# Second MoE stage: a GpSimd drain between scatters, an earlier load of the rare path's flag, and branch hints

## The chip, the cores and the metric

The kernel runs on one core of one Trainium2 chip. Its time is the device time of one execution in microseconds (us), lower is better. Engines: TensorE (PE, with its weight loads PEld), VectorE (DVE), ScalarE (ACT), GpSimd (POOL), SyncE (SP). SyncE and GpSimd issue the DMA transfers.

## What is computed

A gated linear recurrence over 768 steps, then two mixture-of-experts stages over the same 3072 rows of 384. Only the second one and the end of the program matter here:

```python
def _moe2_ref(x, w_skip, w_gate, w1, w2) -> np.ndarray:
    ...
    skip_score = x @ w_skip
    do_compute = skip_score > 0
    out = x.copy()
    ...
    for e in range(E):                      # 8 experts
        mask = e_idx == e
        ...
        h = np.maximum(xc[mask] @ w1[e], 0.0)
        y[mask] = gate_w[mask, None] * (h @ w2[e])
    out[do_compute] = xc + y
    return out.astype(np.float32)
```

## The kernel before

The recurrence is done first, in chunks of 128 steps; the first MoE stage follows and writes its rows to the output in DRAM; the second MoE stage updates those rows in place.

The second stage (`Moe2`, line 1476) works in 8 slots, numbered 0 to 7 here, one expert each, on one tile of 128 rows that were gathered from the output. `Rows128.run` (line 1288) writes out the order of every slot by hand, and `tc.manual_schedule()` (line 1567) keeps it: each engine runs its instructions in the order in which the program names them. A slot does, in this order: `ahead(s)` (loads), the first half of the first product, the first half of the second product of the slot before, the second half of the first product, the transposes, the second half of the second product of the slot before, and `finish(s - 1)`. Between them the weights of the next slot are split into a high and a low part in eight pieces, ScalarE making the high part (line 144) and VectorE the low one by a subtraction (line 145). So the scatter of slot s stands near the end of slot s + 1, and the last slot's two half products follow behind the loop.

`Moe2.finish` (line 1497) makes `z` on VectorE (line 1500, a tile with two buffers) and issues the scatter of `z` to the output on GpSimd (line 1502). Every scatter waits for the landing of the one before, since both write the output. There are eight scatters, one for each slot; no other transfer is issued on GpSimd in the stage.

`Moe2.run` (line 1506) takes one `hook`, which its `ahead` calls at slot 2, behind that slot's loads: the function `remaining` (line 1807), a few VectorE instructions that count what does not fit into the eight slots and leave it as an integer in `tot`.

Behind the stage a rare path stands in the program, for data that do not fit: the recurrence once more step by step, more slots of both stages. It is some thousands of instructions long. The branch around it is

```python
        with tc.If(flag(tot, 0, 4) > 0):
```

(line 1830). `flag` (line 1827) is `nc.values_load`, which makes all five engines load `tot` into a register (line 1828) behind nine instructions that each wait for one or two semaphores; then each engine branches. With these data `tot` is 0, so every engine jumps over the rare path to the end of the program. [...]

Of the kernel before, what the change touches and what calls it, by code (L numbers as in the profile page):

```python
# [16 lines left out]
PSUM = bass.MemoryType.PSUM  # L17
DRAM = bass.MemoryType.DRAM
IDX = bass.IndirectOffsetOnAxis

B, H, S, D = 4, 8, 768, 48
N, DM, E, F = 3072, 384, 8, 1024
# [32 lines left out]
KP, SP = (3, 4, 5), ()  # L55
# [43 lines left out]
class Weights:  # L99
# [3 lines left out]
    W = 3 * F + 8 * DW  # L103
# [12 lines left out]
    def load_rows(self, s, w1, w2, idx, wg=None):  # L116
        for o, w, n in ((3 * F + 8 * DM, wg, 8 * RC), (0, w1, 3 * F), (3 * F, w2, 8 * DM)):
            if w is not None:
                self.nc.gpsimd.indirect_dma_start(
                    out=self.raw[s % 2][:, o:o + n], out_offset=None, in_=w, in_offset=IDX(ap=idx, axis=0),  # L120
                    bounds_check=E * 128 - 1, oob_is_err=False)
# [1120 lines left out]
class Rows128:  # L1242
# [45 lines left out]
    def run(self, slots, src, ahead, fill, finish, x=None, side=lambda: None):  # L1288

        slots = list(slots)  # L1290
        x = x or self.turn(src(slots[0]))
        prev = None
        for i, s in enumerate(slots):
            ahead(s)
            f = fill(s)
            h0 = self.half1(s, x, 0)
            side()
            if prev is not None:
                self.half2(s - 1, prev, 0)
            next(f, None)  # L1300
            next(f, None)
            side()
            h1 = self.half1(s, x, 1)
            if i + 1 < len(slots):
                x = self.turn(src(s + 1))
            hs = [self.turn_h(h0)]
            next(f, None)
            next(f, None)
            side()
            if prev is not None:  # L1310
                finish(s - 1, self.half2(s - 1, prev, 1))
            hs.append(self.turn_h(h1))
            emit(f)
            side()
            prev = hs
        self.half2(s, prev, 0)
        finish(s, self.half2(s, prev, 1))


class Moe1:  # L1320
# [34 lines left out]
    def gather_rows(self, out, c, n=N):  # L1355
        self.nc.gpsimd.indirect_dma_start(
            out=out, out_offset=None, in_=self.k.x0[0:n], in_offset=IDX(ap=self.R.idx[:, c:c + 1], axis=0),
            bounds_check=n - 1, oob_is_err=False)
# [48 lines left out]
    def finish(self):  # L1407
        emit(self.side)
# [7 lines left out]
    def store(self, c, ps):  # L1416
# [5 lines left out]
        nc.gpsimd.indirect_dma_start(  # L1422
            out=k.out, out_offset=IDX(ap=R.idx[:, c:c + 1], axis=0), in_=y, in_offset=None,
            bounds_check=N - 1, oob_is_err=False)
# [51 lines left out]
class Moe2:  # L1476
# [20 lines left out]
    def finish(self, s, ps):  # L1497
# [4 lines left out]
        nc.gpsimd.indirect_dma_start(  # L1502
            out=k.out, out_offset=IDX(ap=k.idx2[:, s:s + 1], axis=0), in_=z, in_offset=None,
            bounds_check=N - 1, oob_is_err=False)

    def run(self, slots, load, loaded=False, hook=None):


        slots = list(slots)
        s0, end = slots[0], slots[-1] + 1  # L1510
        if not loaded:
            for s in range(s0, min(s0 + 2, end)):
                load(s)
                self.gather(s)
            emit(self.W.split(s0))
        else:
            for s in range(s0 + E - 2, end):
                self.gather(s)

        def ahead(s):  # L1520
            if s + 2 < end:
                if not loaded:
                    self.gather(s + 2)
                load(s + 2)
            if hook is not None and s == s0 + 2:
                hook()

        def fill(s):
            return self.W.split(s + 1) if s + 1 < end else iter(())

        self.rows.run(slots, lambda s: self.xg[s % E], ahead, fill, self.finish)
# [3 lines left out]
def tile_lru_attention_moe_moe(  # L1535
# [19 lines left out]
    nc = tc.nc  # L1555
    k = Env()
# [10 lines left out]
    with tc.manual_schedule():  # L1567
# [71 lines left out]
        W = Weights(nc)  # L1639
# [58 lines left out]
        tot = ct([1, 2], "tot2", I32)  # L1698
        R2 = Router(nc, k, const2, rt1, SUB1, "b")

        xq = [xg0[:, 0], xg0[:, 1], *(ct([128, DM], f"xq{i}") for i in range(2, E - 2))]
# [115 lines left out]
            v.tensor_tensor(rest[:, 0:1], rest[:, 0:1], rest[:, 1:2], op=ALU.add)  # L1817
            v.tensor_copy(tot[:, 0:1], rest[:, 0:1])

        def second_moe(ctx):  # L1820
            Moe2(nc, tc, k, W, ctx, xq, gather2).run(range(E), lambda s: W.load(s, v1, v2, s), loaded=True, hook=remaining)

        for moe in (first_moe, second_moe):
            with ExitStack() as c:
                moe(c)

        def flag(x, i, n):
            return nc.values_load(x[:, i:i + 1], min_val=0, max_val=n)

        with tc.If(flag(tot, 0, 4) > 0):  # L1830
            with tc.If(flag(k.okn, 0, 2 * 128 * G) < 2 * 128 * G):
                attention_steps(nc, tc, k)
                with ExitStack() as c:
                    sp = c.enter_context(tc.tile_pool(name="sl_s", bufs=1))
                    ps = c.enter_context(tc.tile_pool(name="sl_q", bufs=1, space=PSUM)).tile([128, 512], F32, name="sps")
                    R1.reset()
                    emit(R1.batch1(0, BT[0], ps))
                    emit(R1.batch1(BT[0], BT[1], ps))
                    emit(early(lambda shape, nm, dt: sp.tile(shape, dt, name=nm), ps[:, 256:]))
                    emit(split0())  # L1840
                for moe in (first_moe, second_moe):
                    with ExitStack() as c:
                        moe(c)
            with tc.If(flag(R1.tot, 3, 2) > 0):
                with ExitStack() as c:
                    m1 = Moe1(nc, tc, k, W, R1, c, xg0)
                    emit(R1.late_tables(m1.acc, c.enter_context(tc.tile_pool(name="m1s", bufs=2)), FIX1, SUB1 - FIX1))
                    with tc.If(flag(R1.tot, 0, 1) > 0):
                        m1.run_more(
                            range(NS1, NSMAX1), lambda s: W.load_rows(s, w1, w2, R1.wix[:, s + NZ1:s + NZ1 + 1], k.wg))  # L1850
                    for i, zs in ((1, range(NZ1, NZ1 + 2)), (2, range(NZ1 + 2, NZMAX1))):
                        with tc.If(flag(R1.tot, i, 1) > 0):
                            m1.run_more_small(
                                zs, lambda z: W.load_rows(z, w1, w2, R1.wix[:, NSMAX1 + z:NSMAX1 + z + 1], k.wg))
                    emit(batch2(FIX1, SUB1, m1.side_ps, None))
            with ExitStack() as c:
                m2 = Moe2(nc, tc, k, W, c, xq, gather2)
                rp = c.enter_context(tc.tile_pool(name="r3", bufs=1))
                pp = c.enter_context(tc.tile_pool(name="r3p", bufs=1, space=PSUM))
                n2 = overflow(nc, k, R2, tot, rp, pp)  # L1860
                for s0 in range(0, J2, 6):
                    with tc.If(n2 > s0):
                        m2.run(
                            range(E + s0, E + min(s0 + 6, J2)),
                            lambda s: W.load_rows(s, v1, v2, k.wix2[:, s - E:s - E + 1]))
# [106 lines left out]
```

## Time and profile before

| | us |
|---|---|
| median of 3 runs (lowest, highest) | 719.96 (714.34, 720.8) |
| the profiled execution | 717.57 |
| its span, first to last instruction | 715.8 |

Busy time in the span: TensorE 610.0 us (85%), VectorE 579.1 (81%), ScalarE 431.4 (60%), GpSimd 208.7 (29%). These are sums over stages with different limits, so they do not say what the end of the program costs. Busy time leaves out what a sequencer does by itself: waits for semaphores, loads of registers, branches and drains. Such instructions stand in the views under the name of their engine with a q (POOLq, DVEq, PEldq, SPq).

### The profile page before, as it was taken

What the parts mean: (1) busy time and instruction counts of PE and PEld (TensorE: products, weight loads), DVE (VectorE), ACT (ScalarE), POOL (GpSimd) and SP (SyncE); (2) the same over time, 40 slices, a digit from 0 to 9 for tenths busy, and PEclk for the clock granted to TensorE, in tenths of its full rate; (3) what the DMA queues carried; (4) which work ended last, traced back from release to release, by engine and by line L of the source; (5) the groups of instructions that cost most, each with busy time, mean ns of one, the idle gap of its engine ahead of it and who ended that gap; (6) DMA issues with size and microseconds to landing.
All of it is one profiled execution on the core that took longest, in us unless ns stands there. A gap on an engine that the chain in (4) does not pass through costs nothing.

```text
span 715.8 us, 13793 instructions
## 1 busy us (share of the span) xinstructions
PE 610.0 (85%) x5015; PEld 527.7 (74%) x5015; DVE 579.1 (81%) x1391; ACT 431.4 (60%) x863; POOL 208.7 (29%) x300
## 2 busy tenths in 40 slices
PE   0788886607999999998698999999999999799991
PEld 0454444406888888887598899999999997588890
DVE  5999999998999989998679666667766678699970
ACT  7767786634656656654543655566555566588860
POOL 6200000002223322234144534445454442601110
PEclk9999998965899999999789999999999999999996
DMA  6759864102998989767250211551111185578800
GB/s 224 285 191 288 289 200 114 66 0 65 244 255 227 229 218 232 194 175 242 91 202 23 66 46 38 224 210 50 34 52 41 33 334 228 214 276 312 312 18 11
DMA packets 39833, 117.21 MB, mean 164 GB/s; under 512 B 10172, under 2 KB 26186, under 8 KB 35404
## 3 DMA queue, kind: packets, MB, share of 16 engines
q1 hardware_dynamic: 22892, 66.37, 29.9%
q0 software_dynamic: 13984, 45.94, 20.5%
q10 hardware_dynamic: 2880, 3.93, 1.8%
q8 instruction: 41, 0.67, 0.4%
q14 instruction: 36, 0.29, 0.1%
HBM read 116.84 MB, written 16.52 MB: 186 GB/s over the span
## 4 chain that ended last, share of the span: by engine, by line
PE 32%; DMA 7%; issue 6%; DVE 6%; POOL 1%; ACT 1%; POOLq 0%; ACTq 0%; DVEq 0%
PE hps L1387 13%; PE yps L1434 13%; DMA out_dram<-z,idx 6%; PE yps L1283 1%; PE hps L1263 1%; DMA P<-in_w_dram,wix 1%; DVE wlo L145 1%; PE xtp L1371 1%; DVE w L145 1%; POOL xq L1704 1%; DMA xq<-out_dram,idx 1%; PE acc L1033 0%; DVE hl L1394 0%; DVE ro L1051 0%; PE yp L644 0%
## 5 line engine op out<-in xcount | busy, mean ns | idle before, releaser
L145 DVE TENSOR_TENSOR wlo<-wraw,whi 128x768 fp32r<-128x768 f32 (+1 forms) x95 | 82.4, 904 | 11.6 <-ACT whi L144 10.8
L145 DVE TENSOR_TENSOR w<-P,w 128x768 fp32r<-128x768 f32 (+1 forms) x95 | 82.6, 906 | 8.7 <-ACT w L144 7.9
L462 POOL DMA_DIRECT2D X<-X x36 | 17.8, 501 | 241.9 <-DVE X L521 226.4
L1394 DVE SCALAR_TENSOR_TENSOR hl<-hps,hh 128x512 fp32r<-128x512 f32 x48 | 33.1, 689 | 54.3 <-ACT hh L1393 47.5
L274 PE MATMUL m<-sq,idn 128*128 128x288 f32 x112 | 39.0, 476 | 42.1 <-ACT sq L267 42.1
L144 ACT ACTIVATE w<-P 128x768 fp32r<-128x768 f32 (+1 forms) x95 | 70.8, 800 | 2.8 <-DMA P<-in_w_dram,wix 2.8
L144 ACT ACTIVATE whi<-wraw 128x768 fp32r<-128x768 f32 (+1 forms) x95 | 71.0, 803 | 0.0
L1393 ACT ACTIVATE hh<-hps 128x512 fp32r<-128x512 f32 x48 | 28.7, 599 | 67.6 <-PE hps L1387 51.0
L274 PEld LDWEIGHTS m<-sq,idn 128*128 128x128 f32 x112 | 21.9, 214 | 54.9 <-ACT sq L267 29.3
L377 DVE TENSOR_TENSOR t<-P,n 128x288 f32<-128x288 f32 x127 | 58.9, 464 | 2.8 <-DVE n L327 0.2
L1422 POOL DMA_INDIRECT out_dram<-y,idx x26 | 30.9, 1187 | 101.9 <-ACT y L1421 98.2
L570 PE MATMUL sc<-X 48*128 48x128 f32 x768 | 56.0, 295 | 0.0
L570 PEld LDWEIGHTS sc<-X 48*128 48x128 f32 x768 | 50.8, 203 | 5.0 <-issue 3.1
L1434 PE MATMUL yps<-w,hh 128*128 128x394 f32 x192 | 51.0, 346 | 0.0
L1387 PE MATMUL hps<-xh,w 128*128 128x256 f32 x288 | 45.1, 289 | 2.6 <-ACT xh L1373 1.4
L1387 PEld LDWEIGHTS hps<-xh,w 128*128 128x128 f32 x288 | 39.7, 194 | 3.5 <-ACT xh L1373 1.8
L574 DVE TENSOR_TENSOR sm<-sc,tri 128x512 f32<-128x512 f32 x48 | 32.1, 685 | 10.8 <-PE sc L570 10.8
L382 DVE TENSOR_TENSOR P<-t 128x144 f32<-128x144 f32 x127 | 39.3, 309 | 0.1
L642 PE MATMUL yp<-sm,v 128*64 128x128 f32 (+1 forms) x384 | 36.2, 277 | 0.0
L1434 PEld LDWEIGHTS yps<-w,hh 128*128 128x128 f32 x192 | 34.9, 189 | 0.0
L274 PE MATMUL u<-sq,idn 128*128 128x288 f32 x112 | 34.9, 438 | 0.0
L1434 PE MATMUL yps<-whi,hh 128*128 128x394 f32 x96 | 33.6, 350 | 0.0
(365 smaller groups left out, 1743.9 us busy)
## 6 DMA issues: line engine op xcount, KB each, us to landing
P<-in_w2t_dram SPq DMA_DIRECT2D x8, 1536.0 KB, 6.7
P<-in_v_dram SPq DMA_DIRECT2D x8, 1536.0 KB, 7.3
wraw<-in_v_dram SPq DMA_DIRECT2D x8, 1536.0 KB, 7.7
qst<-X SPq DMA_DIRECT2D x48, 192.0 KB, 6.7
raw<-in_a_dram SPq DMA_DIRECT2D x15, 576.0 KB, 6.0
v<-in_v_dram POOLq DMA_DIRECT2D x12, 384.0 KB
out_dram<-xg SPq DMA_DIRECT2D x12, 384.0 KB, 5.9
q<-in_q_dram POOLq DMA_DIRECT2D x11, 384.0 KB
```

The lines of the kernel that those rows point to most:

```text
L144: self.nc.scalar.activation(out=hi, in_=r, func=AF.Copy)
L145: self.nc.vector.tensor_tensor(lo, r, hi.bitcast(F32), op=ALU.subtract)
L274: nc.tensor.matmul(x, k.idn, sq[:, h, :, r], start=r == 0, stop=last and r == 1)
L377: nc.vector.tensor_tensor(t1, P.at(t - 1)[:, ::-1].unsqueeze(2).to_broadcast([128, 2, 2, G]), pairs, op=ALU.mult)
L382: nc.vector.tensor_tensor(P.at(t), t1[:, 0], t1[:, 1], op=ALU.add)
L570: nc.tensor.matmul(ps[:, pair], kk, q, start=r == 0, stop=r == 1)
L574: nc.vector.tensor_tensor(X[i].sm[:, 4 * g:4 * g + 4], X[i].sc[g], k.mask.to_broadcast([128, 4, 128]), op=ALU.mult)
L642: nc.tensor.matmul(o, U[n].v[:, c, h * 48:h * 48 + M], x.sm[:, 4 * par + pair], start=zero, stop=True)
L1387: nc.tensor.matmul(ps[:, i], self.W.w1(s, wp_, j)[:, f * 128:f * 128 + 128], x[xp_][:, j], start=n == 0, stop=n == 8)
L1394: nc.vector.scalar_tensor_tensor(out=hl, in0=ps, scalar=0.0, in1=hh.bitcast(F32), op0=ALU.max, op1=ALU.subtract)
L1422: nc.gpsimd.indirect_dma_start(out=k.out, out_offset=IDX(ap=R.idx[:, c:c + 1], axis=0), in_=y, in_offset=None, bounds_check=N - 1, oob_is_ ...
L1434: nc.tensor.matmul(ps, hs[kk // 2][hp][:, kk % 2, us], self.W.w2(s, wp_, kk, Weights.DW), start=n == 0, stop=n == 23)
```

## The change

`Moe2.run` takes a table of hooks by slot in place of one. `remaining` stays at slot 2. At slot 3 GpSimd gets a drain instruction; in GpSimd's order it stands behind the scatter of slot 1 and ahead of that of slot 2. At slot 5 the flag is loaded on all engines, in place of behind the stage. At slot 6 each engine gets a branch hint for the branch with the label "more", with 0 as the value it is to be prepared for; a `no_sync_barrier` ahead of it marks the place in the order and is no instruction. The branch around the rare path gets that label and takes the value loaded at slot 5.

```diff
+ENGINES = [getattr(mybir.EngineType, e) for e in ("PE", "DVE", "Activation", "Pool", "SP")]
...
-    def run(self, slots, load, loaded=False, hook=None):
+    def run(self, slots, load, loaded=False, hooks={}):
...
-            if hook is not None and s == s0 + 2:
-                hook()
+            if s - s0 in hooks:
+                hooks[s - s0]()
...
-        def second_moe(ctx):
-            Moe2(nc, tc, k, W, ctx, xq, gather2).run(range(E), lambda s: W.load(s, v1, v2, s), loaded=True, hook=remaining)
-
-        for moe in (first_moe, second_moe):
-            with ExitStack() as c:
-                moe(c)
-
         def flag(x, i, n):
             return nc.values_load(x[:, i:i + 1], min_val=0, max_val=n)
 
-        with tc.If(flag(tot, 0, 4) > 0):
+        more = []
+
+        def second_moe(ctx, hooks=None):
+            Moe2(nc, tc, k, W, ctx, xq, gather2).run(
+                range(E), lambda s: W.load(s, v1, v2, s), loaded=True, hooks={2: remaining, **(hooks or {})})
+
+        with ExitStack() as c:
+            first_moe(c)
+        def hint():
+            tc.no_sync_barrier()
+            tc.mark_branch_hint_location("more", 0, ENGINES)
+
+        with ExitStack() as c:
+            second_moe(c, {3: nc.gpsimd.drain, 5: lambda: more.append(flag(tot, 0, 4)), 6: hint})
+
+        with tc.If(more[0] > 0, label="more"):
```

## Rows read from the trace of the kernel before

**Rows 1.** Busy time by stretch: slots, then the end; columns as headed.

```profile
core 0: us, PE busy (x) PEld busy (x) DVE busy (x) ACT busy (x) POOL busy (x), PEclk, DMA share, GB/s
648.50:658.15 9.65, 9.43 (x52) 8.62 (x53) 9.37 (x13) 7.64 (x13) 0.99 (x1) 1.00 0.85 308
667.77:677.40 9.63, 9.63 (x55) 8.68 (x54) 9.36 (x13) 8.43 (x14) 0.97 (x1) 1.00 0.93 329
...
700.50:715.80 15.30, 0.00 (x0) 0.00 (x0) 0.00 (x0) 0.00 (x0) 0.97 (x1) 0.60 0.03 10
```

**Rows 2.** Timeline from 699.4: start, us, instruction, [idle before, releaser].

```profile
699.88 0.62 DVE L1500 SCALAR_TENSOR_TENSOR z<-zps,gate,xq 128x384 f32<-128x384 f32 x1 [2.89 <-PE zps L1283]
700.77 0.97 POOL L1502 DMA_INDIRECT out_dram<-z,idx  x1 [3.67 <-DVE z L1500]
```

**Rows 3.** Line 1828, the flag: count, duration ns min/median/max, first and last start.

```profile
L1828 PEldq EVENT_SEMAPHORE  x9: 51/51/51, 697.1 to 698.0; - x9
L1828 DVEq EVENT_SEMAPHORE  x9: 49/50/50, 699.9 to 700.7; - x9
L1828 POOLq EVENT_SEMAPHORE  x9: 43/43/43, 700.5 to 701.5; - x9
...
L1828 DVEq TENSOR_LOAD <-tot x1: 546/546/546, 700.8 to 700.8; - x1
```

**Rows 4.** Line 1830, the branch.

```profile
L1830 POOLq EVENT_SEMAPHORE  x6: 17/30/43, 705.5 to 706.0; - x6
...
L1830 PEldq COMPARE_BRANCH  x1: 3345/3345/3345, 698.7 to 698.7; - x1
...
L1830 POOLq COMPARE_BRANCH  x1: 62/62/62, 702.2 to 702.2; - x1
L1830 POOLq INC_SWDGE_SEM  x1: 1881/1881/1881, 706.1 to 706.1; - x1
```

**Rows 5.** Line 1958, the end of the program.

```profile
L1958 SPq EVENT_SEMAPHORE  x14: 17/28/28, 707.9 to 715.7; - x14
...
L1958 POOLq DRAIN  x3: 46/103/6934, 708.0 to 715.5; - x3
L1958 SPq DRAIN  x3: 7/7/7, 708.7 to 715.2; - x3
```

**Rows 6.** DMA packets from 704.1 to the end.

```profile
DMA packets 2, 0.02 MB, mean 1 GB/s; under 512 B 0, under 2 KB 0, under 8 KB 0
## 3 DMA queue, kind: packets, MB, share of 16 engines
q14 instruction: 2, 0.02, 0.5%
```

**Rows 7.** Line 1967, the start of the program.

```profile
L1967 POOLq INC_SWDGE_SEM  x1: 27/27/27, 0.2 to 0.2; - x1
...
L1967 POOLq DRAIN  x1: 184/184/184, 0.4 to 0.4; - x1
```

**Rows 8.** GpSimd's groups of transfers, first and last of 20.

```profile
L1422 POOL DMA_INDIRECT out_dram<-y,idx x26 | 30.9, 1187 | 101.9 <-ACT y L1421 98.2 <-ACT hrow L1266 3.0 <-ACT rs_ex L926 0.7
...
L1655 POOL DMA_DIRECT2D bi<-in_bias_dram x1 | 0.6, 569 | 0.0
```

**Rows 9.** Chain that ended last: start, us, flights of the scatters of slots 1, 2, 5, 6.

```profile
649.48 6.76 DMA out_dram<-z,idx
...
659.10 8.62 DMA out_dram<-z,idx
...
687.97 2.15 DMA out_dram<-z,idx
...
696.12 2.89 DMA out_dram<-z,idx
```

**Rows 10.** Timeline of VectorE where hook 5 falls.

```profile
672.43 1.82 DVE L145 TENSOR_TENSOR w<-P,w 128x768 fp32r<-128x768 f32 x2
674.49 0.56 DVE L1254 TENSOR_TENSOR zl<-tp,zh 128x384 fp32r<-128x384 f32 x1 [0.24 <-ACT zh L1253]
...
677.45 0.61 DVE L1500 SCALAR_TENSOR_TENSOR z<-zps,gate,xq 128x384 f32<-128x384 f32 x1
```

**Rows 11.** Timeline of TensorE where the next slot begins.

```profile
676.46 1.64 PE L1263 MATMUL gps<-w,zh 128*128 128x512 f32 x6
```

**Rows 12.** DMA queues from 676.5 to 699.

```profile
q8 instruction: 1, 0.02, 0.3%
```

## Prediction before the run

> **What bounds the kernel now.** I read the end first, because the change touches nothing ahead of the second MoE stage, and then the slots of that stage, because it puts instructions into them. The stretches of that stage show what each slot is made of: TensorE is busy for 9.63 of a slot's 9.63 us and VectorE for 9.36 of it, while GpSimd works for 0.97 us, one scatter [rows 1]. So TensorE paces the slots, VectorE has hardly any room, and GpSimd has more than 8 us of it. The last stretch is another thing: 15.3 us with no TensorE, VectorE or ScalarE work at all and one GpSimd instruction [rows 1]. These 15.3 us of 715.8 are what the change is aimed at.
>
> The timeline of the end gives its beginning: the last `z` runs from 699.88 to 700.50, and the scatter that writes it is issued from 700.77 to 701.74 [rows 2]. What follows are sequencer instructions, which the busy times leave out; the views by source line show them, one line each for the flag, the branch and the end of the program.
>
> - Line 1828, the flag: every engine takes nine waits and one load of `tot`. On GpSimd the waits run from 700.5 to 701.5 [rows 3].
> - Line 1830, the branch: GpSimd branches at 702.2, the branch itself is 62 ns, and its next instruction starts at 705.5, so 3.3 us pass in which nothing waits for data. TensorE's own branch takes 3.35 us in its record, which is the same gap seen from inside. Then six waits until 706.1, the last four of them on the scatters' semaphores, then INC_SWDGE_SEM, 1.88 us [rows 4].
> - Line 1958, the end: GpSimd's DRAIN from 708.0, 6.93 us. Beside it SyncE takes its last waits from 707.9 to 708.7, 0.8 us. After the DRAIN, at 714.9, two short barrier rounds lead to 715.8, 0.85 us [rows 5].
>
> So the path behind the last scatter is: branch gap, landing of the scatter, six waits, INC_SWDGE_SEM, DRAIN, barrier; and GpSimd carries all of it.
>
> **The drain between scatters.** What does the 6.93 us DRAIN do? It is not waiting for data: no scatter packet moves after 704.1, only two packets of instructions [rows 6], and it starts at 708.0. It is not a fixed price either: the DRAIN at the program's start takes 184 ns and the two behind the long one 103 and 46 ns; INC_SWDGE_SEM takes 27 ns at the start and 1881 ns at the end [rows 5, 7]. Between the cheap and the dear ones stand 205 GpSimd transfers (20 groups, 26 the largest, 1 the smallest) [rows 8]. I read the price as one per transfer since the last drain: 6.93 / 205 = 34 ns each, and 9 ns each for INC_SWDGE_SEM. The new drain is issued by hook 3, behind the scatter of slot 1 and ahead of that of slot 2. Six scatters follow it, so the final DRAIN should cost 0.2 to 0.4 us and INC_SWDGE_SEM 0.03 to 0.25 us; I take 0.3 and 0.2. The bounds of the gain are nothing (the new drain settles nothing that the last one would do) and all but these.
>
> With DRAIN at 0.3 us, SyncE's 0.8 us of waits end last. So the step from INC_SWDGE_SEM's end to the barrier falls from 6.9 to 0.8: 6.1 us gained. INC_SWDGE_SEM gives 1.7.
>
> The new drain itself costs about what the old one did, up to 199/205 of 6.93 = 6.7 us. Queued behind it on GpSimd is the scatter of slot 2 (659.10), and only VectorE's `z`, which has two buffers, waits for scatters. If the drain also waits for the scatter in flight (649.48, landing 6.76 us later at 656.2), it ends at 663.0 and slot 2's scatter is 4 us late; with its 8.62 us of flight [rows 9] it lands at 671.8, and the `z` that takes its buffer back is written at 677.45 [rows 10]: 5.6 us to spare. I cost it at nothing.
>
> **The flag ahead of the end.** Hook 5 puts nine waits and a load on each engine into slot 5. At the end it moves GpSimd's branch from 702.2 to 700.6, since its sequencer reaches the nine waits at 700.5. In slot 5 it is new work. On VectorE the nine waits and the load last from 699.9 to 701.3, 1.4 us [rows 3]; they fall ahead of the subtraction at 672.43. Subtractions start 0.87 us apart and the sequencer gets on when the one before starts, so 0.55 us shows. The 0.24 us of idle time ahead of `zl` at 674.49 takes part back [rows 10]. The other 0.3 us reaches TensorE, whose six matmuls with `w` start at 676.46 and need the subtractions that end just then [rows 11]. TensorE's nine waits stand at 697.1 to 698.0, while `z` still waits for its matmuls until 699.88 [rows 2, 3]; so TensorE had 2.8 us of work queued when it took them, which covers the waits and a load like VectorE's, 1.5 us. ScalarE has 1.2 us of idle time in that slot and GpSimd 8.6 [rows 1]; SyncE has issued its last weights by then. I take 0.4 us lost; the bounds are 0 and 1.5 (no cover on TensorE at all).
>
> **The hints.** One more sequencer instruction per engine, two at most. The nearest rows are an event wait (17 to 51 ns) and a load of 546 ns [rows 3, 4]; TensorE's queue covers either, VectorE has idle time in the last slot. Bounds 0 and 0.5 us, taken as nothing. Hook 6 runs as slot 6 of 0 to 7 begins, some 20 us ahead of GpSimd's branch. If the gap of 3.3 us goes, GpSimd stands at its scatter waits by 701.5, and then the landing ends last: the scatter before it needed 2.89 us from issue, the one before that 2.15 [rows 9]; with 2.89 this one lands at 703.7. The last four of the six waits then take 0.35, so INC_SWDGE_SEM starts at 704.0 in place of 706.1: 2.1 us gained. Bounds: 1.1 (landing when its packets now end, 704.1, with 0.6 us more) and 2.8 (2.15 us).
>
> [...]
>
> **The sum**, against the profiled execution, 717.57 us with 715.8 of span: 6.1 + 1.7 + 2.1 - 0.4 = 9.5 us less, 708.1. Checked forward: 703.7 landing, 704.0, INC_SWDGE_SEM to 704.2, SyncE to 705.0, barrier to 705.9, with 0.4 added 706.3 of span and 1.8 around it, 708.1. The median of the runs shown, 719.96, lies 2.4 us above the profiled execution, which by the same 9.5 gives 710.5. I forecast 709.0, between the two.
>
> **The rivals.**
> A. *The drain settles nothing in advance.* The final DRAIN would stay 6.9 us and INC_SWDGE_SEM 1.9, either because they go by all transfers of the program or because something else than transfers is paid there. For it: the trace of before has no drain in mid-program. Against it: 103 and 46 ns right behind the long one. Left are 2.1 - 0.4 = 1.7 us: 715.9, or 718.3 from the median; within 1%.
> B. *The hint does not do what it says.* GpSimd still loses 3.3 us behind its branch, but the branch stands at 700.6, so it is back at 703.9, and two waits on, at 704.1, it finds the scatter landed. That is 0.4 us later than in the forecast: 709.4. The flag's move alone gives most of what the hint could, so this hardly shows in the time.
> C. *Slower: the drain in slot 3 is held up by VectorE.* At the end of the program the 6.93 us pass with VectorE idle; in slot 3 VectorE is busy 9.37 of 9.65 us [rows 1]. If GpSimd gets on only in VectorE's gaps, the drain stretches. The place is the scatter of slot 2; it delays `z` at 677.45 once the drain lasts over 677.45 - 8.62 - 656.2 = 12.6 us, and from there every us is one on the path. At 22 us the gain of 9.5 is gone, and at 29 us, four times its length, the kernel is 1% slower: about 727. Against it: scatters are issued in 0.97 us in a slot with VectorE busy and at the end with VectorE idle alike [rows 1, 2]. [...]
>
> **How the numbers follow.** The forecast's mechanism, with or without a working hint (B), 0.75 (B about 0.15 of it); A 0.18; C 0.05; 0.02 for a mixture. A measurement of this kernel can tell about 1%, 7.2 us of 719.96, from no change; the runs shown lie 6.5 us apart. The forecast's 9.5 us clears the 1% by 2.3 only, so of its 0.75 I give 0.60 to faster and 0.15 to no change; A goes to no change, C to slower, the mixture to either side: 0.61 faster, 0.33 within 1%, 0.06 slower. The range goes from 704.5 (2.8 for the landing and no loss in slot 5 give 707.0, less most of the 3.2 us by which the lowest run shown lies under the profiled one) to 716.0, which takes in A by its own time; the forecast alone has 705.5 to 712.5.
>
> **What would show it.** Right: a DRAIN of about 6 to 7 us on GpSimd between 650 and 663, and at line 1958 one under 0.8 us; INC_SWDGE_SEM under 0.3 us; under 0.5 us between GpSimd's branch and its next instruction; the last stretch of 15.3 us down to about 5.5. Wrong: a last DRAIN still near 7 us (A); 3 us behind the branch (B); scatters of slots 3 to 6 late by more than 5 us, or gaps of TensorE in slots 5 to 7 (C, or the flag's cost mis-sized).

## The result, and the profile after

The changed kernel takes 708.75 us (median of 4 runs, 707.97 to 710.9) against 720.38 us for the kernel before, timed beside it: ratio 0.9842, 95% interval 0.9804 to 0.988, that is 8.6 to 14.1 us less. Timed again beside the last experiments it takes 711.0 against 721.58: 0.9858, 0.9815 to 0.9901. The forecast of 709.0 us lay 0.25 us above the first median and 2.0 under the second; it was set between 708.1 and 710.5, so the first closeness is partly luck.

The profiled execution of the changed kernel took 708.59 us, with a span of 706.9; before it was 715.8. So the span is 8.9 us shorter. To see where, the same three stretches as in [rows 1], shifted to the same places by `z`, the third from the beginning of the last `z`:

```profile
core 0: us, PE busy (x) PEld busy (x) DVE busy (x) ACT busy (x) POOL busy (x), PEclk, DMA share, GB/s
649.36:659.01 9.65, 9.43 (x52) 8.63 (x53) 9.39 (x13) 7.66 (x13) 0.99 (x1) 1.00 0.88 318
668.63:678.86 10.23, 10.23 (x57) 9.24 (x56) 9.40 (x13) 8.47 (x14) 3.50 (x1) 1.00 0.89 313
701.28:706.87 5.59, 0.00 (x0) 0.00 (x0) 0.62 (x1) 0.00 (x0) 0.97 (x1) 0.76 0.06 21
```

The first line, the slot with the new drain, is as long as before. The second, the slot with the flag, has grown from 9.63 to 10.23 us; measured from `z` to `z` (668.69 to 678.86) it is 10.17 in place of 9.62, 0.55 more. The third has the last `z` in it (0.62); behind its end 4.97 us are left where there were 15.3 [rows 1]. That is 10.3 us less. The balance: 10.3 at the end, less 0.55 in the slot of the flag, less 0.86 that the stage began later in this execution (first `z` at 638.71 in place of 637.85, where both kernels run the same code), is the 8.9 of the span. That start wanders from execution to execution (640.29 in the next profile of the changed kernel), so single spans say little here, and the experiments below are read by the end and by the slots. "The end" always means the time from the end of the last `z` to the end of the program.

The lines by which the end shrank, in the view by source line of the changed kernel (line, engine, operation, count, duration ns min/median/max, first and last start in us). The branch, for [rows 4]:

```profile
L1839 POOLq EVENT_SEMAPHORE  x6: 17/30/43, 702.5 to 704.9; - x6
L1839 ACTq EVENT_SEMAPHORE  x2: 17/17/17, 699.7 to 699.8; - x2
...
L1839 ACTq COMPARE_BRANCH  x1: 68/68/68, 697.1 to 697.1; - x1
L1839 PEldq COMPARE_BRANCH  x1: 407/407/407, 698.5 to 698.5; - x1
L1839 DVEq COMPARE_BRANCH  x1: 90/90/90, 701.3 to 701.3; - x1
L1839 POOLq COMPARE_BRANCH  x1: 74/74/74, 701.9 to 701.9; - x1
L1839 POOLq INC_SWDGE_SEM  x1: 312/312/312, 705.0 to 705.0; - x1
```

The end of the program, for [rows 5], and the new drain in its slot:

```profile
L1967 SPq EVENT_SEMAPHORE  x14: 17/28/28, 705.2 to 706.8; - x14
...
L1967 POOLq DRAIN  x3: 52/109/542, 705.3 to 706.6; - x3
L1967 SPq DRAIN  x3: 7/7/7, 706.0 to 706.3; - x3
```

```profile
L1527 POOLq DRAIN  x1: 12327/12327/12327, 650.1 to 650.1; - x1
```

The last DRAIN is 0.54 us in place of 6.93, INC_SWDGE_SEM 0.31 in place of 1.88, and GpSimd is at its next instruction 0.5 us after it reaches the branch, in place of 3.3. The new drain stands in the record for 12.3 us, from 650.1, when the scatter of slot 1 is still being issued, to 662.4. Two things were not in the forecast: ScalarE still takes 2.6 us from its branch (697.1) to its next instruction (699.7) although it was given a hint, and the scatters behind the drain take up to 3.5 us to issue (below).

### The profile page after: what moved, and what is told of

The parts are those of the page before. It is cut to its first block, busy times and chain, and to the rows that moved or that the text cites. A ratio compares the mean times of both kernels' runs of the same rounds, so it can differ in the third digit from the quotient of the medians.

```text
span 706.9 us, 13799 instructions
## 1 busy us (share of the span) xinstructions
PE 611.0 (86%) x5015; PEld 528.8 (75%) x5015; DVE 579.6 (82%) x1391; ACT 431.2 (61%) x863; POOL 215.6 (30%) x300
## 4 chain that ended last, share of the span: by engine, by line
PE 51%; DVE 23%; ACT 12%; issue 7%; DMA 6%; POOL 1%; SPq 0%; POOLq 0%; ACTq 0%; DVEq 0%
PE yps L1435 12%; PE hps L1388 11%; PE sc L571 5%; PE m L275 3%; DVE t L378 3%; PE gps L1264 3%; DVE w L146 2%; PE ktp L558 2%; PE zps L1284 2%; DVE wlo L146 2%; PE yp L645 2%; DVE P L383 2%; PE yp L643 2%; ACT sq L268 2%; PE wps L600 1%
## 5 line engine op out<-in xcount | busy, mean ns | idle before, releaser
L645 PE MATMUL yp<-qst,Ssb 96*48 96x128 f32 (+1 forms) x320 | 34.3, 293 | 0.0
```

The costliest lines, as they stand in the source:

```text
L645: nc.tensor.matmul(o, x.sb[:, pair, 64 * par:64 * par + M], U[n].qst[:, h, cs], start=True, stop=False)
```

## The experiments

All kernels below compute the whole result. Where a ratio is given with its interval, it rests on several executions; the others have one time and one profile, and what follows from them rests on the profile.

### One part at a time

Theory: the drain gives some 8 us at the end, the flag and the hints together 2, and the parts add. Rival: the parts overlap, so that one of them alone gives nearly all.

The drain alone, flag and branch where they were:

```diff
-            second_moe(c, {3: nc.gpsimd.drain, 5: lambda: more.append(flag(tot, 0, 4)), 6: hint})
+            second_moe(c, {3: nc.gpsimd.drain})
-        with tc.If(more[0] > 0, label="more"):
+        with tc.If(flag(tot, 0, 4) > 0, label="more"):
```

> Only the drain at slot 3 is left of the change; the flag is loaded behind the stage and there is no hint. Theory (the drain's price is paid per GpSimd transfer since the last drain, and the flag and the hint are worth little): GpSimd branches near 2.3 us behind the start of the last z, loses about 3.3 us, then INC_SWDGE_SEM 0.3, SyncE's waits 0.8, barriers 0.85: from the end of the last z to the end of the program about 7.5 us (15.3 before, 5.0 in the changed kernel). No loss in slot 5, so z follows z at 9.63 us there. Time about 7.7 us under before, ratio 0.989. Rival (the drain alone does nothing, flag and hint make the gain): the last DRAIN stays near 6.9 us and the ratio is 0.998 to 1.0.

Measured: ratio to the kernel before 0.9858 (0.9819 to 0.9897), 714.07 us against 724.29; the end is 7.24 us. The view by source line:

```profile
L1839 POOLq EVENT_SEMAPHORE  x6: 17/30/43, 706.9 to 707.4; - x6
...
L1839 PEldq COMPARE_BRANCH  x1: 3542/3542/3542, 700.2 to 700.2; - x1
...
L1839 POOLq COMPARE_BRANCH  x1: 62/62/62, 703.8 to 703.8; - x1
L1839 POOLq INC_SWDGE_SEM  x1: 312/312/312, 707.5 to 707.5; - x1
```

```profile
L1967 POOLq DRAIN  x3: 46/103/537, 707.8 to 709.1; - x3
```

The gap behind the branch is whole (703.8 to 706.9), the DRAIN is short: 15.3 - 7.24 = 8.0 us come from the drain alone.

The flag and the hints without the drain:

```diff
-            second_moe(c, {3: nc.gpsimd.drain, 5: lambda: more.append(flag(tot, 0, 4)), 6: hint})
+            second_moe(c, {5: lambda: more.append(flag(tot, 0, 4)), 6: hint})
```

> Flag at slot 5 and hint at slot 6, no drain. Theory: the last DRAIN is 6.9 us and INC_SWDGE_SEM 1.9 us again; from the end of the last z to the end 12.7 us (15.3 before, 5.0 changed), slot 5 longer by 0.5; time about 2 us under before, ratio 0.997. All scatters are issued in 1.0 us (in the changed kernel those of slots 2, 3 and 4 took 3.0 to 3.5). Rival (flag and hint make the gain): ratio 0.985 to 0.99.

Measured: ratio 0.9967 (0.9928 to 1.0006), 721.6 against 724.29. The end is 13.02 us, with DRAIN at 6.93 and INC_SWDGE_SEM at 1.88 as before: 2.25 us come from the flag and the hints together. All scatters are issued in 0.97 to 1.01 us.

```profile
L1839 POOLq INC_SWDGE_SEM  x1: 1881/1881/1881, 708.7 to 708.7; - x1
```

```profile
L1967 POOLq DRAIN  x3: 46/109/6929, 710.6 to 718.1; - x3
```

The changed kernel without the hints:

```diff
-            second_moe(c, {3: nc.gpsimd.drain, 5: lambda: more.append(flag(tot, 0, 4)), 6: hint})
+            second_moe(c, {3: nc.gpsimd.drain, 5: lambda: more.append(flag(tot, 0, 4))})
```

> Drain at slot 3 and flag at slot 5, no hint. Theory: TensorE's branch record is 3.3 us again and GpSimd's gap behind its branch 3.3 us instead of 0.5; as the branch stands right behind the last z, GpSimd is back 0.9 us after the last scatter has landed: from the end of the last z to the end 5.9 us instead of 5.0, time 0.9 us over the changed kernel, ratio to before 0.985 to 0.986. Rival (the hint is what removes the gap of the end): 2.8 us over the changed kernel. Rival (the hint does nothing and the short gap has another cause): gap still 0.5, tail 5.0.

Measured: ratio 0.984 (0.9788 to 0.9891); the end is 5.54 us.

```profile
L1839 POOLq EVENT_SEMAPHORE  x6: 17/30/43, 706.5 to 707.0; - x6
...
L1839 PEldq COMPARE_BRANCH  x1: 3466/3466/3466, 700.0 to 700.0; - x1
...
L1839 POOLq COMPARE_BRANCH  x1: 62/62/62, 703.5 to 703.5; - x1
```

GpSimd loses 3.0 us behind the branch again (703.5 to 706.5), but its branch now stands beside the last scatter's start (703.7), and when it comes back the scatter has landed: its wait for it costs nothing. So the early flag on top of the drain is worth 7.24 - 5.54 = 1.7 us, and the hints on top of both 0.3 to 0.6 (5.54 against 5.22 and 4.97 in the two profiles of the changed kernel; the 0.25 between these two is the landing, 2.73 and 2.48 us behind the issue by GpSimd's wait). These steps add up by the way they are taken. The test of whether the parts add is the kernel without the drain: 8.0 for the drain alone and 2.25 for the rest alone make 10.3, and both together gave 10.0 and 10.3. So the rival is refuted.

### Whom a hint helps

In the changed kernel the hint shortened GpSimd's and TensorE's gaps, not VectorE's and ScalarE's. The DMA records of instruction packets suggest why: between hint and branch there is one packet for GpSimd (692.7) and one for TensorE (679.0), while ScalarE's and VectorE's last ones (649.5 and 661.7) were already there when their hints ran (678.2 and 681.7). The records name a packet's queue and not its engine, so the engines are ascribed here by when the packets come, which is an estimate. (For GpSimd's there is a check: in the kernel with the drain in the last slot, below, GpSimd stands until 700.6, and that packet comes at 701.5.) Theory: a hint acts only when a packet of instructions for its engine follows it. Rival: it does not work on these two engines at all. The hint moved to slot 1, ahead of those packets:

```diff
-            second_moe(c, {3: nc.gpsimd.drain, 5: lambda: more.append(flag(tot, 0, 4)), 6: hint})
+            second_moe(c, {1: hint, 3: nc.gpsimd.drain, 5: lambda: more.append(flag(tot, 0, 4))})
```

> The changed kernel with the hint at slot 1 instead of slot 6. In the changed kernel the gap behind the branch is short on GpSimd (0.5 us) and on TensorE (record 0.4 us) but 2.6 us on ScalarE and 2.9 us on VectorE. Theory: a hint acts only when the engine fetches its next block of instructions between hint and branch; GpSimd (packet at 692.7) and TensorE (679.0) did, ScalarE (last one near 649.5) and VectorE (near 661.7) had done so before their hints at 678.2 and 681.7. With the hint at slot 1 both gaps fall to about 0.5 us; the time stays within 0.5 us, as neither engine ends last. If the hinted block takes the place of the next one, TensorE, which fetches several blocks between slot 1 and the branch, stalls once by about 3 us and the time rises by that. Rival (the hint acts through the engine, or through the time left, not through a fetch): ScalarE and VectorE keep 2.6 and 2.9 us.

Measured: ratio 0.9843 (0.9809 to 0.9877), the end 5.23 us.

```profile
L1839 ACTq EVENT_SEMAPHORE  x2: 17/17/17, 702.4 to 702.5; - x2
L1839 DVEq EVENT_SEMAPHORE  x2: 21/21/21, 706.7 to 706.8; - x2
...
L1839 ACTq COMPARE_BRANCH  x1: 68/68/68, 701.8 to 701.8; - x1
L1839 PEldq COMPARE_BRANCH  x1: 407/407/407, 703.2 to 703.2; - x1
L1839 DVEq COMPARE_BRANCH  x1: 90/90/90, 706.0 to 706.0; - x1
```

ScalarE is back 0.55 us after its branch in place of 2.6, VectorE 0.55 in place of 2.9; TensorE keeps its short branch (0.41 us in its record) although three packets ascribed to it came in between. SyncE kept a gap of some 5 us, which costs nothing, as it branches 31 us ahead of the end. That agrees with the theory too: the queue of these engines' packets has only two between SyncE's hint (638.8) and its branch (680.4), at 655.7 and 666.0, the ones ascribed to ScalarE and VectorE. Nor is it the time from hint to branch that decides: SyncE's hint had 42 us here and did nothing, while in the changed kernel GpSimd's worked with 19 and VectorE's failed with 20. The end did not get shorter by the early hints: nothing at the end waits for ScalarE and VectorE.

### What a transfer costs at the next drain

The forecast's price was 34 ns for each transfer since the last drain, from one point. If it holds, a drain in the middle of the first MoE stage, with 55 transfers behind it, leaves a final DRAIN of 0.05 + 55 x 0.034 = 1.9 us (the text below counts some 70 transfers and starts from the 542 ns measured with six: 2.4 to 2.8).

```diff
                 fill = W.split(s + 1, True)
+                if s == 6:
+                    nc.gpsimd.drain()
...
-            second_moe(c, {3: nc.gpsimd.drain, 5: lambda: more.append(flag(tot, 0, 4)), 6: hint})
+            second_moe(c, {5: lambda: more.append(flag(tot, 0, 4)), 6: hint})
```

> The changed kernel with its drain moved ahead to slot 6 of the first MoE stage; some 70 GpSimd transfers then follow it (205 in the program). Theory (a price per transfer since the last drain, from 542 ns with 6 of them and 6934 ns with 205, so 32 ns each and 350 ns at the least): the last DRAIN is 2.4 to 2.8 us and INC_SWDGE_SEM 0.7 to 0.9 us. Rival (any drain in the program makes the last one short): DRAIN 0.5 us. Rival (only the kind of the transfers counts, indirect ones being dear): the last DRAIN is above 4 us. The drain itself stands among gathers that the first stage needs, so the time may be worse by some us; that is not what it is for.

A miss: the final DRAIN took 4.54 us and INC_SWDGE_SEM 1.29, far above either; the end is 10.04 us, the time 714.98 (before 717.48). Above 4 us was the sign of the last rival, that only transfers with indices are dear. All 55 behind this drain have indices, so it is not settled here; the drain ahead of both stages, below, answers it.

```profile
L1969 POOLq DRAIN  x3: 52/109/4544, 707.8 to 712.9; - x3
```

A second drain, ahead of the last two scatters:

```diff
-            second_moe(c, {3: nc.gpsimd.drain, 5: lambda: more.append(flag(tot, 0, 4)), 6: hint})
+            second_moe(c, {3: nc.gpsimd.drain, 5: lambda: more.append(flag(tot, 0, 4)), 6: hint, 7: nc.gpsimd.drain})
```

> The changed kernel with a second drain at slot 7, behind the scatter of slot 5 and ahead of that of slot 6. Theory: the second drain settles four transfers (slots 2 to 5); if a drain waits for the transfer in flight it lasts until that has landed, about 2.2 us, else 0.5 us; the last DRAIN has two transfers and takes 0.4 us. In the changed kernel the three scatters behind the drain took 3.0 to 3.5 us to issue instead of 1.0: if that comes from the drain, the scatters of slots 6 and 7 take 3 us too and the time rises by 2 to 2.5 us; if it comes from that place in the program, they take 1.0 us and the time stays.

Measured: 712.8 us (before 717.48); final DRAIN 0.21 us, INC_SWDGE_SEM 0.23, the end 4.88. The second drain, with four transfers to settle, still took 2.59 us: it ended 0.5 us behind the last packet of the scatter that was in flight. So it waited for the transfer in flight. (The last kernel below has such a second drain too: 3.54 us for three transfers, ended 0.6 behind the last packet.) The scatters behind it were issued in 0.97 us, so it holds up nothing else.

The only drain in the last slot:

```diff
-            second_moe(c, {3: nc.gpsimd.drain, 5: lambda: more.append(flag(tot, 0, 4)), 6: hint})
+            second_moe(c, {5: lambda: more.append(flag(tot, 0, 4)), 6: hint, 7: nc.gpsimd.drain})
```

> The changed kernel with its drain at slot 7 instead of slot 3: 203 transfers ahead of it, two behind. Theory: it takes 7 to 9 us (12.3 us at slot 3, where the scatter in flight needed 8 us to land and VectorE was busy; 6.9 us at the end of before), the scatter of slot 6 is issued up to 1 us late, the last DRAIN takes 0.4 us. If a drain slows the scatters behind it, those of slots 6 and 7 take 3 us and the time is 2 to 2.5 us over the changed kernel. If VectorE stretches a drain (the slower rival of the prediction), it lasts above 10 us here too.

Measured: 712.49 us (before 717.48); the drain lasts 7.98 us in the record, 6.78 behind the end of the issue that it follows (5.9 behind that scatter's last packet), and ends at 700.58. The scatter of slot 6 is issued at 701.79, 0.8 us later behind its `z` than usual, and the end is 5.43 us. So the drain costs nothing even here, but there is no room left: the place in slot 3 is the safe one.

Over the kernels' final drains the price is a straight line, except for the kernel before (durations in ns, from the same two lines of each profile):

```
transfers since the last drain   final DRAIN   INC_SWDGE_SEM
  2  (two drains)                     211            232
  2  (drain in the last slot)         222            232
  3  (all parts placed, below)        298            247
  6  (the changed kernel)             542            312
 55  (drain in the first stage)      4544           1292
107  (drain ahead of the stages)     8793           2332
205  (the kernel before)             6934           1881
```

From 2 to 107 it is (8793 - 211) / 105 = 82 ns for each transfer at DRAIN and (2332 - 232) / 105 = 20 ns at INC_SWDGE_SEM; 3, 6 and 55 lie on these lines within 6 ns. All the transfers counted there, up to 107, have indices; of the 205, 95 have none. The 205 of before fit neither: by both lines 6934 and 1881 are 84 transfers. When only the points up to 55 were known, this left two readings, and a drain between the recurrence and the first MoE stage tells them apart:

```diff
         def gather0():
+            nc.gpsimd.drain()
...
-            second_moe(c, {3: nc.gpsimd.drain, 5: lambda: more.append(flag(tot, 0, 4)), 6: hint})
+            second_moe(c, {5: lambda: more.append(flag(tot, 0, 4)), 6: hint})
```

> One drain on GpSimd between the recurrence and the first MoE stage, with 98 transfers ahead of it (95 plain ones and 3 with indices) and 107 behind it, all with indices; none in the second stage. With 2, 6 and 55 transfers behind the last drain the final DRAIN took 0.21, 0.54 and 4.54 us, that is 0.055 + 0.081 per transfer; the 205 of the kernel before fit only 85 by that. Theory 1 (every transfer costs the same, and some of them are settled without a drain once about 120 have gathered): the new drain takes about 8 us, the final DRAIN 8.7 and INC_SWDGE_SEM 2.3. Theory 2 (the number that settles by itself goes by their place in the program, not by the last drain): new drain 8 us or less, final DRAIN 6.9 and INC_SWDGE_SEM 1.9 as in the kernel before. Theory 3 (the plain transfers of the recurrence cost next to nothing, only those with indices count): new drain under 0.5 us, final DRAIN 6.5 to 8.7.

```profile
L1840 POOLq INC_SWDGE_SEM  x1: 2332/2332/2332, 708.7 to 708.7; - x1
```

```profile
L1968 POOLq DRAIN  x3: 52/109/8793, 711.1 to 720.4; - x3
```

The first theory's numbers for the end (8.7 and 2.3) came, to 0.1 us. The new drain itself can't be read as cleanly: it stands in the record for 17.1 us from 331.8, when two transfers and six other GpSimd instructions ahead of it were still to come, and ends at 348.9, 10.4 us behind the last of them and 4.5 behind the last packet of a transfer; about 8 was expected. Under 0.5 us, as by the third theory, it was not, although 95 of the 98 transfers ahead of it have no indices: so these cost too. The final DRAIN is longer than without any drain, with half as many transfers since the last one, and the end is 15.3 us, beside 13.0 with the same flag and hints and no drain, so this drain gains nothing: 722.4 us, one execution beside one of the kernel before of 717.43. In that place it also holds up the first gather of the stage, issued at 349.9 in place of 344.2. The reading that fits, an estimate from the two lines, is that without a drain some 205 - 84 = 121 of the 205 are settled on the way, and that a drain starts that count anew. Where on the way, and at what number, was not tried; two other durations agree with it, though: in the kernel with the drain in the first stage, 150 transfers stood ahead, 150 - 121 = 29 times 82 ns is 2.4 us, and it took 2.59; in the last-slot kernel 203 stood ahead, 82 x 82 ns = 6.7, and it took 6.78 behind the scatter.

### What stretched the drain in slot 3

In slot 3 the drain was in the record for 9.6 to 12.3 us, in all kernels that have it there. Either it waits for the scatter in flight first, or VectorE's work stretches it, which is rival C. Here the drain stands behind a small GpSimd copy of `z`, so that the scatter of slot 1 has landed when it starts, and VectorE is as busy as before:

```diff
     def finish(...):
...
+        if s == 2:
+            nc.gpsimd.tensor_copy(self.probe, z[:, 0:1])
+            nc.gpsimd.drain()
...
-            second_moe(c, {3: nc.gpsimd.drain, 5: lambda: more.append(flag(tot, 0, 4)), 6: hint})
+            second_moe(c, {5: lambda: more.append(flag(tot, 0, 4)), 6: hint})
```

> The changed kernel with its drain moved: GpSimd first copies a column of z of slot 2, which it can do only once that z is written, then drains, then issues the scatter of slot 2. By then the scatter of slot 1 has landed, and VectorE is busy as before. Theory 1 (the drain of slot 3 lasted 10 to 12.3 us because it first waited for the scatter in flight): the drain lasts 6.5 to 7.2 us, as at the end of the program before. Theory 2 (VectorE's work or the weights' transfers stretch it): 9 to 11 us or more. The last DRAIN has six or seven transfers behind the new drain either way: 0.5 to 0.6 us.

```profile
L1506 POOLq DRAIN  x1: 6674/6674/6674, 664.6 to 664.6; - x1
```

6.67 us, with the copy (0.18 us) in it: 6.5 for the drain, beside 78 x 82 ns = 6.4 by the price with 199 transfers ahead and 121 settled. With VectorE as busy as in the 9.6 to 12.3 us, it was not VectorE that stretched the drain but the flight. What is left open is how flight and settling overlap: with the scatter in flight the drain ended 3.7 to 4.4 us behind its last packet, not 6.5, so by this estimate part of the settling ran beside the flight.

### What the flag costs in slot 5

The slot of the flag was 0.55 us longer in the changed kernel's first profile and 0.15 longer in the experiments with the flag there (9.73 to 9.79 from `z` to `z`). Without the flag (the drain alone) it is 9.62. The flag moved to the middle of the same slot:

```diff
+        def side():
+            seen.append(0)
+            if mid is not None and len(seen) == 4 * 5 + 2:
+                mid()
...
-            second_moe(c, {3: nc.gpsimd.drain, 5: lambda: more.append(flag(tot, 0, 4)), 6: hint})
+            second_moe(c, {3: nc.gpsimd.drain, 6: hint}, lambda: more.append(flag(tot, 0, 4)))
```

> The changed kernel with the flag loaded in the middle of slot 5, behind the first half of the second product, instead of at its start. In the changed kernel TensorE reaches the nine waits only 1.4 us ahead of the work that they hold up and takes 1.9 us for them and the load, so slot 5 is 0.54 us longer. Theory: in mid-slot TensorE has more work queued and the slot stays at 9.63 us: z to z 9.63 instead of 10.17, time 0.5 us under the changed kernel. Rival (VectorE's 1.4 us of waits and load is what lengthens the slot): z to z stays 10.0 to 10.2.

Measured: the slot is 9.63 us, so nothing is lost there; the end 5.22, the time 714.77 (before 717.48; its stage began 4.8 us later than in the repeat of the changed kernel, below, with the same code ahead). The rows of the flag in the two profiles of the unaltered changed kernel show what made 0.55 of 0.15, first profile first:

```profile
L1822 PEldq EVENT_SEMAPHORE  x9: 51/51/51, 666.3 to 667.2; - x9
...
L1822 PEldq TENSOR_LOAD <-tot x1: 861/861/861, 667.3 to 667.3; - x1
```

```profile
L1822 PEldq EVENT_SEMAPHORE  x9: 51/51/51, 667.9 to 668.8; - x9
...
L1822 PEldq TENSOR_LOAD <-tot x1: 487/487/487, 668.9 to 668.9; - x1
```

TensorE's sequencer stood for 1.9 us the first time (666.3 to 668.2) and 1.5 the second. The matmuls `gps` behind the load started 0.90 us behind the start of the transposes ahead of them in the first profile (668.25, below), 0.50 in the second, 0.36 in the kernel before: 0.54 and 0.14 us late, which is the slot's whole loss both times, and ahead of VectorE's waits (from 671.6). The experiment moved the flag on all engines, so it is these rows that tell TensorE's sequencer from VectorE. It had only some 1.4 us of work queued here (1.9 - 0.54, 1.5 - 0.14), not 2.8. The load of 861 ns came once in all the profiles with an early flag; why is open.

```profile
667.35 0.60 PE L1274 MATMUL tp<-idn,h 128*128 128x128 f32 x4
668.25 0.93 PE L1264 MATMUL gps<-whi,zh 128*128 128x512 f32 x3 [0.30 <-issue]
```

### The changed kernel again, and all parts in their best places

> The changed kernel once more, unaltered, beside the next one. Theory 1: the scatters of slots 2 to 4 with 3.0 to 3.5 us of issue and TensorE's flag load of 861 ns belonged to one profiled execution. Then the scatters take 0.97 us, the load 0.48 to 0.50 us, slot 5 lasts 9.76 to 9.79 from z to z, the tail behind the last z about 5.0 us. Theory 2: they come from the flag and the hints as placed in this kernel. Then they come again, with slot 5 at about 10.1. Time against before: ratio 0.982 to 0.987.

Measured, without any edit: 711.0 against 721.58, ratio 0.9858 (0.9815 to 0.9901); the end 5.22, slot 5 9.77, the load 0.49 us. The first theory holds for the load and fails for the scatters, which were slow again:

```profile
L1503 POOL DMA_INDIRECT out_dram<-z,idx x8: 971/998/3490, 641.2 to 703.4; - x8
```

Those of slots 2 to 4 took 3.49, 2.80 and 2.10 us to issue; 3.01, 3.50 and 3.41 in the first profile. Flag and hint do not make them so by themselves: on GpSimd the first slow one is issued ahead of both, and the kernel with two drains, with the same flag and hints, has none over 1.61. What the seven issues over 2 us in all the profiles share is that each begins 3.8 to 5.2 us behind its `z`, in the midst of VectorE's subtractions, where the drain, or the late landing of the scatter before, has pushed it; the ones that begin 0.9 us behind `z` take 0.97 to 1.01 us. Subtractions alone do not make an issue that long: eleven more begin among them, take 0.99 to 1.75 us and end within 0.03 us of the end of a subtraction. One of these is in the kernel before (678.63 to 680.38):

```profile
L1502 POOL DMA_INDIRECT out_dram<-z,idx x8: 971/972/1746, 638.7 to 700.8; - x8
```

Why seven go on to the end of the series and eleven do not is open.

VectorE's timeline beside the slow one of slot 2, issued from 664.40 to 667.89:

```profile
663.48 1.82 DVE L146 TENSOR_TENSOR w<-P,w 128x768 fp32r<-128x768 f32 x2
665.22 1.82 DVE L146 TENSOR_TENSOR wlo<-wraw,whi 128x768 fp32r<-128x768 f32 x2
667.29 0.56 DVE L1255 TENSOR_TENSOR zl<-tp,zh 128x384 fp32r<-128x384 f32 x1 [0.25 <-ACT zh L1254]
```

The issue ends when the subtractions are over and `zl` has run (667.85); of the seven, six end within 0.1 us of `zl`'s end and one 0.05 us behind its start. This is read from rows and was not tried by an experiment. Against its rival C the prediction had the scatter's 0.97 us with VectorE busy and idle alike, and left out the 1.75 above. Seventeen of these eighteen issues end within 0.1 us of the end of an instruction of VectorE, but in the seven long ones several subtractions end before GpSimd gets on; what holds GpSimd there no run shows. It costs no time here: the `z` that takes the buffer back (678.86 in the first profile) stands 7 us behind the landing (671.7).

Last, the hints at slot 1, drains at slots 3 and 6, the flag in the middle of slot 5:

```diff
-            second_moe(c, {3: nc.gpsimd.drain, 5: lambda: more.append(flag(tot, 0, 4)), 6: hint})
+            second_moe(c, {1: hint, 3: nc.gpsimd.drain, 6: nc.gpsimd.drain}, lambda: more.append(flag(tot, 0, 4)))
```

> The changed kernel with every part put where the runs so far say it costs least: the hint at slot 1, drains at slots 3 and 6, the flag in the middle of slot 5. Theory: slot 5 at 9.62 to 9.64 us from z to z (0.15 less than with the flag at the slot's beginning), last DRAIN about 0.3 us with three scatters behind the last drain, INC_SWDGE_SEM about 0.25, gaps behind the branch under 0.6 us on VectorE and ScalarE, tail 4.8 to 5.2 us. Time 0.2 to 0.6 us under the changed kernel, which the runs cannot tell from nothing. Rival: the last 5 us still go by the price of transfers; then the tail would fall by about 0.3 us against the changed kernel.

Measured: ratio 0.9864 (0.9812 to 0.9916), beside 0.9858 for the changed kernel with the same runs of before: no difference. Slot 5 is 9.62, the final DRAIN 0.30, the gaps 0.55, the end 5.17, as expected, but there was no more than half a microsecond to be had: what ends last is the scatter's landing (2.5 to 2.8 us behind its issue by GpSimd's wait, in all kernels with the early flag and hints), then SyncE's waits and the barriers, 1.6.

## Why the prediction was right

**The drain, forecast 6.1 + 1.7 = 7.8 us.** Right: 8.0 alone (6.2 and 1.6 by the rows; the other 0.2 is a branch gap that was shorter in that profile). The reading that the price goes by the transfers since the last drain holds for every drain that follows another, and so does the end by SyncE's 0.8 us (705.2 to 706.1) once the DRAIN is short. The term that was mis-sized is the price: 34 ns came from dividing by all 205, which by the lines above cost as much as 84; it is 82 ns. The last DRAIN was 0.54 us where 0.2 to 0.4 were forecast, hidden behind SyncE's 0.8, and INC_SWDGE_SEM 0.31, 0.06 beyond its bound. With more than some 8 transfers behind the new drain (705.3 to 706.0, 0.7 us at 82 ns each) the DRAIN would have ended last, and the mis-sized price would have shown.

**The new drain at nothing.** Right, with the end at 662.43 and the scatter at 663.30 where 663.0 was forecast. The steps to it were less good: the flight lasted longer (last packet 658.0 in place of 656.2), and less of the drain came behind it (4.4 us in place of 6.7). That the two errors cancel is luck. (The sum's landing, 663.0 + 8.62, is 671.6 and not 671.8; it came at 671.7 from a later start.) The condition of rival C, a drain stretched by VectorE, is refuted by the drain with no flight, 6.5 us beside a busy VectorE; what was longer among VectorE's subtractions is the issue behind the drain, 3.50 us in place of 0.97 at the most, which the forecast had not; behind that, 7 us were still to spare.

**Hint and landing, forecast 2.1 us.** Right as a sum: 2.25 without the drain, 2.0 to 2.3 with it. It is mostly the flag's: 1.7 for the earlier branch and 0.3 to 0.6 for the hint, landing included, as rival B said (0.4). The landing came 2.5 or 2.7 us behind the issue rather than 2.89. That the hint worked on GpSimd is luck: the forecast had no condition for it, and one more packet of instructions, by its time GpSimd's, happened to come between hint and branch (692.7), where VectorE and ScalarE, hinted in the same slot, had none and kept gaps of 2.9 and 2.6 us. Further packets between hint and branch did not undo the hint: TensorE kept its short branch, 0.41 us, through three in the kernel with the early hint. The other engines had at most one there, so more is not shown for them. In these runs the gap was short, 0.4 to 0.6 us, only where a packet came behind the hint.

**The flag in slot 5, forecast 0.4 us.** The size was in the bounds (0.15 in most profiles, 0.55 in the first), the reason wrong. The step that failed is "TensorE had 2.8 us of work queued": that was read behind the stage's last products, in front of a wait, and in slot 5 it has some 1.4. TensorE's own sequencer lost the time, not VectorE's subtraction.

**Rival A** (the drain settles nothing in advance) is refuted by every kernel with a drain in the second stage. The last stretch, forecast at about 5.5 us, is 4.97, the difference being the landing.

## What to carry to other kernels

Read the sequencer's rows at the end of a program: where GpSimd has issued transfers, DRAIN and INC_SWDGE_SEM there together cost 0.1 us here (82 and 20 ns) for each one since the last drain, and a drain put where GpSimd had 10 us to spare moved that off the path. Put ahead of 107 of the transfers it gained nothing: the final DRAIN took 8.79 us. A price taken from one point is to be tested with a second count of transfers. A flag for a rare path is loaded ahead of the end, in a place where TensorE's sequencer has work queued (0.15 to 0.55 us were lost here at a slot's beginning, nothing in mid-slot), and a hint stands early enough for a packet of instructions to come for its engine between it and the branch: here only such hints shortened the branch, to 0.4 to 0.6 us from 2.4 to 3.5. And read a change of 1% by stretches: the stage of this kernel began anywhere from 638 to 645 us with the same code ahead of it.

## What the runs showed of the hardware

- A GpSimd DRAIN at the end took 82 ns, and INC_SWDGE_SEM 20 ns, more for each GpSimd transfer since the last drain (2 to 107 transfers, all with indices); 205 without a drain cost as much as 84. A drain with a transfer in flight was longer: 2.59 us for four transfers behind a scatter, where the price is 0.33, ending 0.5 us behind the scatter's last packet; 9.6 to 12.3 in the record in slot 3 with a flight, 6.5 us with none and 199 transfers ahead.
- The taken branch over the rare path cost 2.4 to 3.5 us here on ScalarE, VectorE, GpSimd and TensorE, and 0.4 to 0.6 with a hint that a packet of instructions followed, by the engines that the packets' times suggest; the same hint gave little or nothing where none followed (ScalarE 2.4 to 2.7, VectorE 2.9 to 3.1, SyncE over 5).
- The issue of a 128-row scatter on GpSimd took 0.97 us or up to 3.50; all that took longer than 1.05 us began among VectorE's subtractions and ended beside the end of a VectorE instruction (in one case its start).
- A register load of one integer on TensorE's sequencer, with its nine waits, took 1.5 to 1.9 us of it: 0.15 to 0.55 us more than it had queued at a slot's beginning, and nothing was lost in mid-slot.
